# Spreading the softmax statistics of the two forward attention passes, with a longer V lag and three of sixteen K copies on ScalarE

## The chip, the cores and the metric

The kernel runs on one core of a Trainium2 chip; the other cores are idle. The metric is the device time of one execution in microseconds (us), lower is better. All runs below are of one core.

Engine names in the profile: PE is TensorE (matmuls), PEld its weight loads, DVE is VectorE, ACT is ScalarE, SPq is the queue in which SyncE issues loads. "L834" is line 834 of the kernel that the profile belongs to, so the same statement has another number in another kernel.

## The reference

Two layers, each an attention block over a long cache and a squared-ReLU feed-forward block, and then the gradient (vjp) of the whole with respect to everything but one input. Cut to what matters here:

```python
# x: [1, 1, 1024]; 32 query heads, 4 KV heads, 65536 keys, head size 128, bf16
def _A_ref(x, k_cache, v_cache, wq, wo):
    q = heads(x @ wq)
    k = jnp.repeat(k_cache, 8, axis=1);  v = jnp.repeat(v_cache, 8, axis=1)
    scores = jnp.einsum("bhqd,bhkd->bhqk", q, k) * (128 ** -0.5)
    p = _softmax(scores, axis=-1)
    return merge(jnp.einsum("bhqk,bhkd->bhqd", p, v)) @ wo

x = x + _A_ref(_layernorm(x), ...);  x = x + _B_ref(_layernorm(x), ...)   # layer 1
x = x + _A_ref(_layernorm(x), ...);  x = x + _B_ref(_layernorm(x), ...)   # layer 2
_out, _vjp = jax.vjp(_f, A_x, A_k_cache, A_v_cache, A_wq, A_wo, ...)      # and all gradients
```

There is one query token. Each KV head's K and V are read for only eight query rows, so an attention pass does little arithmetic for each byte that it loads.

## The kernel before

The kernel goes over the caches four times: forward of layer 1, forward of layer 2, backward of layer 2, backward of layer 1. Between them lie short "dense" stretches with projections and the feed-forward block. The change is confined to the two forward passes (and one line of the background products that run within them).

K and V come in blocks of 1 MB (128 partitions x 32 rows of 128), often two in one load. All loads go through one in-order queue and wait there until a slot of the on-chip arena is free.

```python
    def kv8(t, g, c8):                       # 8 rows per partition of block (t, g, hb)
        hb, j = divmod(c8, J)                # J = 32
        ...
            if i is None:
                sl = Slot("blk_" + t)
                nc.sync.dma_start(out=sl.t.rearrange("p (j d) -> p j d", d=DH), in_=half(KVIN[t], g, hb))
        ...
        return have[key].t.rearrange("p (j d) -> p j d", d=DH)[:, j:j + 8, :]
```

An *item* is 8 chunks of 128 keys. Sixteen items (128 chunks) make a *unit*, the piece over which one running maximum is taken. A pass has 16 units, so the two forward passes have 32. The pipeline runs three stages for each item, with lags in items:

```python
    FWD_LAG = TLEAD + SU // 8 + 5            # 2 + 16 + 5
    ...
        pipeline(items, [(kT, 0), (kS, TLEAD), (v8, FWD_LAG)], bg, end, holds)
```

`kT` transposes K on PE (eight 128x128 transposes into one PSUM bank), and the bank is copied to SBUF by the helper `evac`. For this kind ("kt") it always takes DVE:

```python
            evac(kt[:, :, :], pt[:, :, :], kind="kt")
```

`kS` makes the scores on PE. At the end of a unit it calls `stats`, which in one go takes the maximum over the unit and over the partitions (with two small PE steps), then eight exponentials on ACT, and then rescales the running sum:

```python
        def stats(g, su):
            ...
            ptm = ps_mv([R, P], F32)
            nc.tensor.transpose(ptm[:, :], pmn[:, :], ident_f[:, :])
            ...                                                  # DVE: min over keys, spread over a tile
            nc.tensor.matmul(pnb[:, :], lhsT=gmb[:, :], rhs=ident_f[0:R, 0:R], start=True, stop=True)
            nc.vector.tensor_copy(out=nm, in_=pnb[:])
            for h in range(R):
                nc.scalar.activation(out=E(p, g, c0, SU)[:, :, h], in_=S[:, h, :], func=ACTF.Exp,
                                     bias=negm[:, g, su, h:h + 1], scale=SCALE, accum_out=rs[:, h:h + 1])
            ...
                nc.scalar.activation(out=al[:], in_=df[:], func=ACTF.Exp)       # after the eight
                nc.vector.tensor_tensor(out=zn[:], in0=state[("z", g)][:], in1=al[:], op=ALU.mult)
                nc.vector.tensor_tensor(out=z2[:], in0=zn[:], in1=rs[:], op=ALU.add)
```

`v8` multiplies V with the exponentials into a PSUM accumulator and, at a unit's end, copies the accumulator out (`oacc`).

## Time and profile before

| | before |
|---|---|
| time, median (range) | 2040.85 us (2039.17 to 2042.13), 3 runs |
| span of the profiled run | 2038.8 us |
| forward pass 1, first transpose to last V product | 18.6 to 378.8 us |
| forward pass 2, the same | 427.6 to 778.6 us |
| rest of the span: backward passes and dense stretches | about 1330 us |

The following lines are the table of stretches of the kernel before: start and end of a stretch, its length, busy time and instructions of each engine, the mean granted PE clock (PEclk), the mean busy share of the core's 16 DMA engines (DMA share; values a little above 1 occur), and the rate.

```profile
core 0: us, PE busy (x) PEld busy (x) DVE busy (x) ACT busy (x) POOL busy (x), PEclk, DMA share, GB/s
20.00:355.00 335.00, 270.37 (x6218) 260.91 (x6216) 201.97 (x436) 92.61 (x286) 0.00 (x0) 0.92 1.01 419
355.00:400.00 45.00, 31.73 (x700) 30.62 (x697) 15.37 (x48) 8.59 (x23) 0.29 (x1) 0.81 0.87 336
400.00:435.00 35.00, 32.17 (x633) 31.12 (x631) 23.30 (x52) 12.86 (x14) 0.55 (x11) 1.00 1.02 403
435.00:455.00 20.00, 18.21 (x461) 17.77 (x457) 16.08 (x31) 7.30 (x20) 0.00 (x0) 1.00 0.43 150
455.00:755.00 300.00, 245.37 (x5611) 236.27 (x5609) 182.45 (x396) 84.06 (x266) 0.00 (x0) 0.91 1.01 419
755.00:790.00 35.00, 24.06 (x541) 23.25 (x538) 10.87 (x35) 7.43 (x22) 0.29 (x1) 0.83 0.73 278
```

The middles of the two forward passes have a DMA share of 1.01 and 419 GB/s. PE is busy 270 of 335 us there (its weight loads, PEld, overlap with that), DVE 202. So these stretches are bound by loading. Several loads are under way at a time: over the whole run a K load of 2 MB takes 19.2 us (median) from issue to landing, while its bytes alone, by my estimate from the 419 GB/s, would take 5 us. "HBM Reference" of the Trainium skill (Specifications) states about 425 GB/s for a core that streams alone, bounded by its 16 DMA engines; this trace agrees with 419. The idle DMA of these 800 us is around the passes' ends and starts (shares 0.87, 0.43 and 0.73).

The next lines are from the list of costliest groups of the kernel before (over the whole span): line, engine, operation, output and input, count, then busy us and mean ns of one, then idle time of the engine just before them and what ended most of it.

```profile
L152 DVE COPY kt<-ps_tr 128x1024 bf16<-128x1024 bf16 x909 | 603.6, 687 | 218.0 <-PE ps_tr L983 99.4
...
L852 PE MATMUL ps_sc<-L_qpad,kt 128*128 128x64 bf16 (+7 forms) x4096 | 206.7, 195 | 51.1 <-DVE kt L152 48.1
...
L149 ACT COPY kt<-ps_tr 128x1024 bf16<-128x1024 bf16 x115 | 114.3, 1013 | 172.4 <-PE ps_tr L983 172.0
```

A K copy costs 0.687 us on DVE and 1.013 us on ACT (ACT does this form in the backward passes already). The scores on L852 show 51.1 us of idle before them, 48.1 of it ended by the K copy.

These are lines of the list of waits of the kernel before, in 20 to 370 us (first pass): who waited for whom, us in total, times, the longest.

```profile
DVE zn L902 <- ACT al L900: 27.6, 8, 4.8
PE ps_sc L852 <- DVE kt L152: 27.5, 15, 3.2
...
DVE zn L902 <- ACT L_fw L938: 8.3, 3, 2.8
```

DVE stood still 27.6 + 8.3 = 35.9 us at the rescaling multiply `zn`, behind the exponentials of ACT. (On ACT's side the releaser is named by the last exponential, al or L_fw; all wait for the same queue of exponentials.)

The two waits hang together. These are lines of the timelines of PE and of DVE in the kernel before, around 105 us:

```profile
106.27 0.41 PE L852 MATMUL ps_sc<-L_qpad,kt 128*128 128x64 bf16 x8 [2.51 <-DVE kt L152]
```

```profile
105.45 0.17 DVE L902 TENSOR_TENSOR zn<-z,al 128x8 f32<-128x8 f32 x1 [2.75 <-ACT L_fw L938]
105.53 0.68 DVE L152 COPY kt<-ps_tr 128x1024 bf16<-128x1024 bf16 x1
```

PE had done its transposes by 103.8 us. DVE stood at `zn` until 105.45 us, then copied K, and the scores began at 106.27.

Finally, two lines of the timeline of PE in the kernel before, one at the end of each forward pass: start, length, what, and in brackets the idle time before it.

```profile
371.79 3.56 PE L917 MATMUL ps_acc<-arena 128*128 128x64 bf16 x64 [5.18 <-ACT L_fw L938]
```

```profile
772.11 2.13 PE L917 MATMUL ps_acc<-arena 128*128 128x64 bf16 x37 [5.18 <-ACT L_fw L938]
```

At each pass's end PE waits 5.18 us for the last unit's exponentials.

### The profile page before, as it was taken

What the parts mean: (1) busy time and instruction counts of PE and PEld (TensorE: products, weight loads), DVE (VectorE), ACT (ScalarE), POOL (GpSimd) and SP (SyncE); (2) the same over time, 40 slices, a digit from 0 to 9 for tenths busy, and PEclk for the clock granted to TensorE, in tenths of its full rate; (3) what the DMA queues carried; (4) which work ended last, traced back from release to release, by engine and by line L of the source; (5) the groups of instructions that cost most, each with busy time, mean ns of one, the idle gap of its engine ahead of it and who ended that gap; (6) DMA issues with size and microseconds to landing.
All of it is one profiled execution on the core that took longest, in us unless ns stands there. A gap on an engine that the chain in (4) does not pass through costs nothing.

```text
span 2038.8 us, 68986 instructions
## 1 busy us (share of the span) xinstructions
PE 1688.1 (83%) x30754; PEld 1358.9 (67%) x30754; DVE 1295.5 (64%) x2742; ACT 956.0 (47%) x1911; POOL 134.6 (7%) x296
## 2 busy tenths in 40 slices
PE   6888888797877886887878888989899979885997
PEld 6777777687877876776867876545555545543554
DVE  4656565466565663455464457868778868874886
ACT  1232232233223223345353446758677757763675
POOL 0000000000000000000000000111111111110121
PEclk8999889899899887988989989989889979996898
DMA  9999999879999997999999985999999999998996
GB/s 390 424 416 419 420 420 416 349 302 422 417 419 420 417 410 290 400 419 415 420 421 420 420 322 217 408 423 411 424 422 424 423 391 406 424 424 362 358 391 246
DMA packets 111544, 802.44 MB, mean 394 GB/s; under 512 B 9472, under 2 KB 9486, under 8 KB 49422
## 3 DMA queue, kind: packets, MB, share of 16 engines
q1 hardware_dynamic: 87198, 632.33, 75.7%
q0 software_dynamic: 24048, 165.70, 19.7%
q8 instruction: 240, 3.93, 0.8%
q14 instruction: 58, 0.48, 0.1%
HBM read 632.30 MB, written 165.69 MB: 391 GB/s over the span
## 4 chain that ended last, share of the span: by engine, by line
PE 52%; DMA 18%; ACT 14%; DVE 10%; issue 5%; SPq 1%; POOL 0%; DVEq 0%; POOLq 0%; ACTq 0%
PE ps_tr L834 9%; DMA arena<-in_A_v_cache_dram 8%; ACT arena L891 6%; DMA out_dram<-arena 5%; PE ps_sc L852 5%; PE ps_acc L917 5%; PE ps_tr L1094 4%; PE ps_gg L1146 4%; PE ps_tr L983 4%; ACT arena L149 4%; DVE kt L152 3%; PE ps_gg L1213 2%; PE ps_sc L1003 2%; PE ps_sc L1127 2%; ACT mv_t L510 2%
## 5 line engine op out<-in xcount | busy, mean ns | idle before, releaser
L152 DVE COPY kt<-ps_tr 128x1024 bf16<-128x1024 bf16 x909 | 603.6, 687 | 218.0 <-PE ps_tr L983 99.4
L149 ACT CAST arena<-ps_gg 128x512 bf16<-128x512 f32 (+1 forms) x893 | 468.5, 599 | 193.2 <-PE ps_gg L1146 167.5
L834 PE MATMUL ps_tr<-ident_b,arena 128*128 128x128 bf16 x4096 | 317.4, 228 | 4.4 <-issue 4.2
L152 DVE CAST arena<-ps_gg 128x512 bf16<-128x512 f32 (+1 forms) x378 | 253.8, 686 | 67.6 <-PE ps_gg L1213 29.0
L834 PEld LDWEIGHTS <-arena 128*128 128x128 bf16 x4096 | 255.3, 103 | 7.1 <-issue 6.7
L852 PE MATMUL ps_sc<-L_qpad,kt 128*128 128x64 bf16 (+7 forms) x4096 | 206.7, 195 | 51.1 <-DVE kt L152 48.1
L1146 PE MATMUL ps_gg<-GG,xt 64*128 64x512 bf16 x1024 | 213.5, 408 | 18.0 <-ACT arena L149 12.3
L856 ACT COPY S_sb<-ps_sc 128x512 f32<-128x512 f32 x64 | 38.5, 602 | 402.0 <-PE ps_sc L852 402.0
L852 PEld LDWEIGHTS <-kt 128*128 128x128 bf16 x4096 | 168.0, 100 | 59.7 <-DVE kt L152 53.6
L917 PE MATMUL ps_acc<-arena 128*128 128x64 bf16 (+4 forms) x4096 | 168.3, 201 | 42.6 <-issue 21.4
L1094 PE MATMUL ps_tr<-ident_b,arena 128*128 128x128 bf16 x2048 | 182.8, 233 | 23.2 <-DMA arena<-in_A_v_cache_dram 20.1
L891 ACT ACTIVATE arena<-S_sb,L_negm 128x128 bf16<-128x128 f32 x256 | 156.0, 1025 | 98.2 <-DVE L_negm L887 98.2
L1094 PEld LDWEIGHTS <-arena 128*128 128x128 bf16 x2048 | 132.0, 104 | 98.1 <-issue 73.2
L149 ACT COPY kt<-ps_tr 128x1024 bf16<-128x1024 bf16 x115 | 114.3, 1013 | 172.4 <-PE ps_tr L983 172.0
L917 PEld LDWEIGHTS <-arena 128*128 128x128 bf16 x4096 | 152.3, 104 | 44.6 <-issue 44.0
L983 PE MATMUL ps_tr<-ident_b,arena 128*128 128x128 bf16 x2048 | 158.4, 228 | 5.2 <-issue 4.2
L1173 PEld LDWEIGHTS <-arena 128*128 128x128 bf16 x2048 | 84.6, 100 | 108.8 <-issue 102.6
L983 PEld LDWEIGHTS <-arena 128*128 128x128 bf16 x2048 | 127.1, 103 | 19.6 <-issue 16.6
L1003 PE MATMUL ps_sc<-dOpad,kt 128*128 128x64 bf16 (+7 forms) x2048 | 107.3, 195 | 34.9 <-DVE kt L152 24.9
L891 ACT ACTIVATION_READ_ACCUMULATOR arena<-S_sb,L_negm 128x1 f32 x256 | 127.4, 497 | 0.0
L1173 PE MATMUL ps_acc<-X,arena 128*128 128x64 bf16 (+3 forms) x2048 | 120.1, 197 | 4.6 <-DMA arena<-in_A_k_cache_dram 4.6
L1127 PE MATMUL ps_sc<-DOB,kt 128*128 128x64 bf16 (+3 forms) x2048 | 117.7, 199 | 0.0
(253 smaller groups left out, 1978.2 us busy)
## 6 DMA issues: line engine op xcount, KB each, us to landing
arena<-in_A_k_cache_dram SPq DMA_DIRECT2D x88, 2048.0 KB, 19.2
arena<-in_A_v_cache_dram SPq DMA_DIRECT2D x83, 2048.0 KB, 22.1
out_dram<-arena POOLq DMA_DIRECT2D x151, 1024.0 KB, 11.5
arena<-in_A_v_cache_dram SPq DMA_DIRECT2D x76, 1024.0 KB, 24.9
arena<-in_A_k_cache_dram SPq DMA_DIRECT2D x72, 1024.0 KB, 24.8
arena<-in_B_w_dram SPq DMA_DIRECT2D x32, 896.0 KB, 7.3
arena<-in_A_wq_dram SPq DMA_DIRECT2D x22, 1024.0 KB, 20.9
arena<-in_B_w_dram SPq DMA_DIRECT2D x21, 1024.0 KB, 9.4
```

The lines of the kernel that those rows point to most:

```text
L149: nc.scalar.copy(out=out, in_=in_)
L152: nc.vector.tensor_copy(out=out, in_=in_)
L834: nc.tensor.transpose(pt[:, i, :], kb8[:, i, :], ident_b[:, :])
L852: nc.tensor.matmul(state["ps_s"][:, s:s + w, :].rearrange("p a b -> p (a b)"), lhsT=kt[:, i, :], rhs=L["qpad"][:, g, 0:w, :].rearrange("p ...
L891: nc.scalar.activation(out=E(p, g, c0, SU)[:, :, h], in_=S[:, h, :], func=ACTF.Exp, bias=negm[:, g, su, h:h + 1], scale=SCALE, accum_out=r ...
L917: nc.tensor.matmul(ps_o[:, 0:w, :], lhsT=vb8[:, i, :], rhs=E(p, g, c, w), start=(c % SU == 0), stop=(c % SU == SU - 1), skip_group_check=True)
L983: nc.tensor.transpose(pt[:, i, :], vb8[:, i, :], ident_b[:, :])
L1003: nc.tensor.matmul(state["ps_dp"][:, s:s + w, :].rearrange("p a b -> p (a b)"), lhsT=vt[:, i, :], rhs=dOpad[:, g, 0:w, :].rearrange("p a b ...
L1094: nc.tensor.transpose(pt[:, i, :], vb8[:, i, :], ident_b[:, :])
L1127: nc.tensor.matmul(state["ps_dp"][:, s:s + w, :].rearrange("p a b -> p (a b)"), lhsT=vt[:, i, :], rhs=DOB[:, g, 0:w, :].rearrange("p a b - ...
L1146: nc.tensor.matmul(pgs[h][:, :], lhsT=xt[64 * h:64 * h + 64, j1 // 8 + m, :], rhs=gg[64 * h:64 * h + 64, :, :].rearrange("p a b -> p (a b) ...
L1173: nc.tensor.matmul(ps_dq[:, 0:w, :].rearrange("p a b -> p (a b)"), lhsT=kb8[:, i, :], rhs=X[:, s:s + w, :].rearrange("p a b -> p (a b)"), ...
```

## The change

The intent is to take stalls out of PE's in-order stream in the forward passes. (1) The chain of the running maximum is spread over the five items that follow a unit, one step behind each item's transposes, so that PE always has other work between the small steps. (2) V runs three items later. (3) The exponential that gives the rescaling factor is issued before the eight long ones, and the rescaling of the sum is written at the unit's end, next to the accumulator's. (4) Three of sixteen K copies go to ACT. (5) One more yield in the background products.

```diff
-        if kind != "kt" and load["act"] + ca <= load["dve"] + cd:
+        if kind == "kta" or kind != "kt" and load["act"] + ca <= load["dve"] + cd:
             nc.scalar.copy(out=out, in_=in_)
 ...
-    FWD_LAG = TLEAD + SU // 8 + 5
+    FWD_LAG = TLEAD + SU // 8 + 8
 ...                                            # background products
+        if ps_of is ps_bg:
+            yield
         finish(ps[:, 0, :])
 ...
+    def after(n, fn):
+        TASKS.setdefault(NOW["i"] + n, []).append(fn)
 ...                                            # pipeline: tasks(i) runs after the first stage of item i
+    ACT_KT = (3, 12, 14)
 ...
-            evac(kt[:, :, :], pt[:, :, :], kind="kt")
+            evac(kt[:, :, :], pt[:, :, :], kind="kta" if c8 % SU // 8 in ACT_KT else "kt")
 ...                                            # kS: the unit's partial maximum
+                def top():
+                    nc.vector.tensor_reduce(out=pm[:, :, h0 // HB], in_=S[:, :, h0:h0 + HB], axis=AX.X, op=ALU.max)
+                after(1, top)
 ...                                            # stats, cut into five functions
+            def exps():
+                nc.vector.tensor_copy(out=nm, in_=v["pnb"][:])
+                if not first:
+                    ...
+                    nc.scalar.activation(out=al[:], in_=df[:], func=ACTF.Exp)
+                ...                             # then the eight exponentials
+            for n, fn in enumerate((lows, turn, low, spread, exps)):
+                after(n + 1, fn)
 ...                                            # v8, at a unit's end
+                    nc.vector.tensor_tensor(out=on[:], in0=ps_o[:, 0, :], in1=t[:], op=ALU.add)
+                    zn = spool.tile([P, R], F32, name="zn", tag="zn")
+                    nc.vector.tensor_tensor(out=zn[:], in0=state[("z", g)][:], in1=al[:], op=ALU.mult)
+                    z2 = spool.tile([P, R], F32, name="z2", tag="z2", bufs=3)
+                    nc.vector.tensor_tensor(out=z2[:], in0=zn[:], in1=rs[:], op=ALU.add)
 ...                                            # the last unit's division, by two more tasks (cut)
```

## The prediction

> **What bounds the kernel now.** The change touches only the two forward attention passes, about 20–379 and 428–779 us of the span (2038.8 us; median time 2040.85 us). The table of stretches shows the 16 DMA engines at share 1.01 and 419 GB/s in 20–355 and 455–755 us. The backward passes, with other compute, reach the same rate (417–424 GB/s), so it is a ceiling. "HBM Reference" of the Trainium skill (Specifications) states about 425 GB/s for a core that streams alone; this trace agrees. PE is busy 81% there, DVE 60%, ACT 28%. So these 635 us are bound by loads of K and V, whose bytes don't change. DMA idles only at the edges: 355–400 us (share 0.87), 435–455 (0.43), 755–790 (0.73), 790–820 (0.86), about 31 us together: an upper limit for the gain, and part of it is the dense phase, which the change leaves.
>
> **What the change does, costed from the trace.** Per unit (16 items; 32 units):
> - Three of 16 K copies move: 3 x 0.69 = 2.1 us less DVE, 3 x 1.01 us more ACT (what ACT takes for this form in the last pass). DVE goes from about 13 to 11 us of a 20 us unit, ACT from 6 to 9. Neither limits.
> - The statistics chain takes 2.0–2.5 us in a row (timeline), PE waiting some 1.1 us in it, then 4.85 us of exponentials. Spread over five items it no longer holds up PE's in-order stream, and three more items of lag (about 1.1 us of PE each) hide the exponentials. The rescaling no longer blocks DVE 2.7 us behind ACT (waits: zn 36 us in the first pass), so K copies and scores (27 us of waits) come sooner.
> - Removed stalls: perhaps 3–4 us of each unit's 20. Almost all turns into waiting for DMA.
>
> **What is on the critical path.** At the end of each forward pass PE waits 5.2 us for the last unit's exponentials (366.6–371.8 and 766.9–772.1 us), its V already landed. With three more items of V to do meanwhile, part is hidden: 1–3.5 us per pass, 2–7 us together. At the start of the second pass (438–453 us) the load queue waits 14 us for slots that V frees after the first exponentials (1.28 us table load, 4.9 us). The spread chain starts them about as late as now, and V starts three items later: between 3 us lost and 2 us won. The start of the first pass is saturated. The extra yield in background products is free.
>
> **Predicted: 2035 us, 8 in 10 within 2018 to 2046.** Faster by over 2%: 0.02; within 2%: 0.97; slower by over 2%: 0.01.
>
> **What would show it.** Middle of the forward passes: DMA share still 1.0, 419 GB/s, same length; PE's waits for K copies and the statistics chain gone, its idle total alike. DVE busy down about 66 us, ACT up about 97 us. PE's wait for the last exponentials of each pass 1–4 us instead of 5.2. First V product of the second pass at about the same time or up to 3 us later, DMA idle in 435–455 us alike. Backward passes alike, only shifted.
>
> **What would make it wrong.** If the scheduler orders PE's stream otherwise and the second pass starts its V products much later, idle DMA grows (5–8 us). If pairs of slots fall otherwise with the longer lag, the in-order load queue could be blocked in mid-pass. If the idle DMA at the edges depends on the stall per unit more than I think, the gain could reach 15–20 us; over 41 us (2%) would need the saturated windows to be not really saturated.

## More of the kernel before

Over both passes, 44.0 of the 48.1 us of waits for K copies are waits during which, for a part, DVE stood at `zn`, and from `zn` on it worked without a pause until the copy was done. No forward transpose of this kernel waits for a load.

## The result, and the profile after

| | before | after |
|---|---|---|
| time, median (range) | 2040.01 us (2037.02 to 2042.13), 4 runs | 2036.47 us (2035.52 to 2041.52), 4 runs |
| ratio after / before | | 0.9989, 95% interval 0.9968 to 1.0010 |
| span of the profiled run | 2038.8 us | 2034.8 us |
| DVE busy / ACT busy | 1295.5 / 956.0 us | 1240.1 / 1049.2 us |

A ratio here is the mean time of one kernel's runs over that of the other's of the same rounds, so it isn't quite the ratio of the medians. The verdict is "same": a change of a tenth of a per cent, with an interval that includes 1. The prediction of 2035 us lies 1.5 us from the median.

The same stretches, in the kernel after:

```profile
20.00:355.00 335.00, 268.93 (x6177) 257.75 (x6175) 177.23 (x390) 137.06 (x331) 0.00 (x0) 0.93 1.01 420
355.00:400.00 45.00, 32.12 (x719) 30.45 (x714) 11.82 (x43) 10.20 (x25) 0.29 (x1) 0.79 0.80 304
400.00:435.00 35.00, 31.65 (x525) 30.84 (x526) 19.31 (x45) 13.42 (x14) 0.55 (x11) 0.88 0.94 373
435.00:455.00 20.00, 19.88 (x469) 19.22 (x467) 16.51 (x32) 8.68 (x16) 0.00 (x0) 1.00 0.68 261
455.00:755.00 300.00, 239.11 (x5733) 228.25 (x5730) 160.12 (x360) 128.79 (x319) 0.00 (x0) 0.96 1.00 416
755.00:790.00 35.00, 24.66 (x593) 23.77 (x590) 9.69 (x34) 9.17 (x24) 0.29 (x1) 0.85 0.90 344
```

The middles are as before: share 1.01 and 1.00, 420 and 416 GB/s. DVE did 25 us less and ACT 44 us more in the first of them, and the DMA share and rate stayed. The ends and starts are mixed: the share falls in 355 to 400 and 400 to 435 us and rises in 435 to 455 and 755 to 790. The stretches are fixed in time while the second pass started 7 us later, so a stretch's share alone says little; the passes' own lengths are better:

| us | pass 1 | dense | pass 2 | dense | backward 1 | dense | backward 2 to the end |
|---|---|---|---|---|---|---|---|
| before | 360.2 | 48.8 | 351.0 | 52.4 | 347.3 | 70.2 | 790.3 |
| before, second profile | 359.9 | 49.5 | 348.3 | 52.7 | 347.4 | 68.4 | 790.7 |
| after | 362.0 | 52.5 | 341.6 | 51.7 | 347.4 | 67.8 | 791.8 |
| after, second profile | 368.2 | 48.4 | 345.6 | 52.2 | 353.3 | 63.7 | 789.9 |

(Passes run from the first transpose to the last V product; the second profiles are of the repeats described below.) The two forward passes sum to 711.2 and 708.2 us before and 703.6 and 713.8 us after. Two profiles of the same kernel differ by 10 us, more than the two kernels do.

The groups after, as shown for the kernel before:

```profile
L152 DVE COPY kt<-ps_tr 128x1024 bf16<-128x1024 bf16 x815 | 546.5, 687 | 288.2 <-PE ps_tr L853 123.9
...
L149 ACT COPY kt<-ps_tr 128x1024 bf16<-128x1024 bf16 x209 | 210.9, 1021 | 375.2 <-PE ps_tr L853 205.2
...
L871 PE MATMUL ps_sc<-L_qpad,kt 128*128 128x64 bf16 (+7 forms) x4096 | 213.1, 195 | 58.1 <-DVE kt L152 43.7
```

DVE has 94 copies of this form less (909 to 815) and ACT 94 more (115 to 209, counted over the whole span, so with those of the backward passes). The edit moves 3 x 32 = 96, and within the forward passes the traces show exactly 96 on ACT; in the backward passes `evac`, which there chooses the engine, gave two copies more to DVE (397 before, 399 after). The scores (L852 before, L871 now) still show 58.1 us of idle, 43.7 of it ended by the K copy.

The waits in 20 to 370 us after:

```profile
PE ps_sc L871 <- DVE kt L152: 24.7, 19, 3.3
DVE z L962 <- ACT arena L929: 22.2, 8, 3.8
...
DVE z L962 <- ACT L_fw L980: 8.1, 3, 2.7
...
PE ps_tr L853 <- DMA arena<-in_A_k_cache_dram: 3.8, 2, 2.3
```

The score products wait 24.7 us for K copies on DVE, against 27.5 before: the wait that the change should have removed is still there. DVE still stands still 22.2 + 8.1 = 30.3 us behind ACT's exponentials. It is only at the add `z` (the z2 of the code) now, and no longer at `zn`. A first direct wait of a transpose for a load shows up as well.

Why does DVE still wait? These two fences are the timeline of DVE around one unit's end, before and after.

```profile
64.08 0.17 DVE L902 TENSOR_TENSOR zn<-rs,al 128x8 f32<-128x8 f32 x1 [3.33 <-ACT al L900]
...
64.76 0.16 DVE L904 TENSOR_TENSOR z<-zn,rs 128x8 f32<-128x8 f32 x1
```

```profile
61.80 0.17 DVE L960 TENSOR_TENSOR zn<-rs,al 128x8 f32<-128x8 f32 x1 [0.40 <-ACT al L924]
64.68 0.17 DVE L962 TENSOR_TENSOR z<-zn,rs 128x8 f32<-128x8 f32 x1 [2.71 <-ACT arena L929]
64.76 0.16 DVE L952 COPY oacc<-ps_acc 128x8 f32<-128x8 f32 x1
```

The kernel text writes `zn` and `z2` after the accumulator's copy `oacc` of their unit. The built program has them in front even of the copy of the unit before: `zn` at 61.80 and `z` at 64.68, then that `oacc` at 64.76. The instruction scheduler had moved them forward when the program was built, and DVE executes in that order. So the add waits 2.71 us for the last of the eight exponentials, as `zn` had waited 3.33 us before, and the copy that frees the PSUM accumulator stands behind it.

Last, the ends of the passes, on PE's timeline after:

```profile
367.66 1.49 PE L945 MATMUL ps_acc<-arena 128*128 128x64 bf16 x29
372.93 1.87 PE L945 MATMUL ps_acc<-arena 128*128 128x64 bf16 x32 [3.78 <-ACT L_fw L980]
```

```profile
765.48 1.01 PE L945 MATMUL ps_acc<-arena 128*128 128x64 bf16 x29
770.74 1.87 PE L945 MATMUL ps_acc<-arena 128*128 128x64 bf16 x32 [4.25 <-ACT L_fw L980]
```

PE still waits for the last exponentials, 3.78 and 4.25 us instead of 5.18. The longer lag leaves V products of the unit before to be done just ahead of the pause (groups of 29), and that makes it shorter, as intended. But in the first pass the 1.4 us didn't shorten the end. The stretches of 4 us there show what else differed, before and then after:

```profile
368.00:372.00 4.00, 0.21 (x5) 0.21 (x5) 0.22 (x2) 3.76 (x16) 0.17 (x1) 0.55 1.01 411
372.00:376.00 4.00, 3.70 (x66) 3.53 (x63) 0.59 (x4) 0.00 (x0) 0.12 (x1) 0.60 0.92 380
376.00:380.00 4.00, 2.96 (x80) 2.76 (x80) 1.48 (x5) 1.87 (x2) 0.00 (x0) 1.00 0.52 213
```

```profile
368.00:372.00 4.00, 1.15 (x25) 1.17 (x23) 0.74 (x5) 3.98 (x16) 0.00 (x0) 0.50 1.02 413
372.00:376.00 4.00, 2.63 (x35) 2.34 (x35) 0.65 (x4) 0.90 (x5) 0.29 (x1) 0.50 0.79 324
376.00:380.00 4.00, 3.77 (x58) 3.29 (x58) 0.87 (x2) 1.87 (x2) 0.00 (x0) 0.50 0.51 210
```

In the kernel after, the granted clock is 0.50 until 381.4 us, 8.5 us past the end of the pause, and in the kernel before only until 375.2 us, 3.4 us past it (ends of the low spells are read from the clock records of the traces). The page "TensorE: Matmul & The Clock Gate" of the Trainium skill (Part 1) says that PE falls to half its clock after an idle window of about 3.4 us, that it needs a busy window of about 3.4 us to come back, and that the windows run freely, whatever the kernel does. The trace agrees in the lengths: the low spells in the forward passes of these two kernels' profiles last 3.4, 6.8, 10.2 or 13.7 us. It doesn't show that the last pause brings the fall: in the kernel after the low clock begins at 367.8 us, before that pause (369.1 us), and of the 24 low spells in the middles of the kernel before none has a pause of PE as long as 3.4 us in the 6.8 us ahead of it. Nor is the long low clock a mark of the change: in the second profile of the kernel before it lasted to 379.1 us, 9.3 us past the pause. The time from last score to last V product was 16.2 and 18.4 us in two profiles of the kernel before and 18.7 and 18.5 after in the first pass; in the second pass 16.1 and 15.3 before, 13.9 and 14.0 after.

At the start of the second pass the load queue waits for the first slots, before and after (issues of SPq, the time of one issue including its wait):

```profile
438.46 14.71 SPq L326 DMA_DIRECT2D arena<-in_A_k_cache_dram  x2
```

```profile
445.35 15.18 SPq L326 DMA_DIRECT2D arena<-in_A_k_cache_dram  x3
```

14.71 against 15.18 us: alike, as predicted. The first V product came 24.1 us after the first transpose before, and 23.3 after.

### The profile page after: what moved, and what is told of

The parts are those of the page before. It is cut to its first block, busy times and chain, and to the rows that moved or that the text cites. A ratio compares the mean times of both kernels' runs of the same rounds, so it can differ in the third digit from the quotient of the medians.

```text
span 2034.8 us, 68978 instructions
## 1 busy us (share of the span) xinstructions
PE 1676.8 (82%) x30754; PEld 1342.9 (66%) x30754; DVE 1240.1 (61%) x2647; ACT 1049.2 (52%) x2008; POOL 134.9 (7%) x296
## 4 chain that ended last, share of the span: by engine, by line
PE 50%; DMA 19%; ACT 16%; DVE 10%; issue 5%; POOL 0%; DVEq 0%; POOLq 0%; ACTq 0%; SPq 0%
DMA arena<-in_A_v_cache_dram 10%; PE ps_tr L853 8%; ACT arena L929 6%; PE ps_sc L871 5%; ACT arena L149 5%; PE ps_acc L945 4%; PE ps_tr L1025 4%; PE ps_gg L1188 4%; PE ps_tr L1136 4%; DMA out_dram<-arena 4%; PE ps_sc L1045 3%; PE ps_gg L1255 2%; DMA arena<-in_A_k_cache_dram 2%; DVE kt L152 2%; ACT kt L149 2%
## 5 line engine op out<-in xcount | busy, mean ns | idle before, releaser
L152 DVE COPY kt<-ps_tr 128x1024 bf16<-128x1024 bf16 x815 | 546.5, 687 | 288.2 <-PE ps_tr L853 123.9
L149 ACT COPY kt<-ps_tr 128x1024 bf16<-128x1024 bf16 x209 | 210.9, 1021 | 375.2 <-PE ps_tr L853 205.2
L853 PEld LDWEIGHTS <-arena 128*128 128x128 bf16 x4096 | 256.6, 103 | 15.5 <-issue 11.1
L871 PE MATMUL ps_sc<-L_qpad,kt 128*128 128x64 bf16 (+7 forms) x4096 | 213.1, 195 | 58.1 <-DVE kt L152 43.7
L871 PEld LDWEIGHTS <-kt 128*128 128x128 bf16 x4096 | 169.5, 100 | 70.2 <-DVE kt L152 51.2
L1136 PEld LDWEIGHTS <-arena 128*128 128x128 bf16 x2048 | 131.8, 104 | 100.6 <-issue 71.8
L945 PE MATMUL ps_acc<-arena 128*128 128x64 bf16 (+4 forms) x4096 | 162.5, 195 | 23.0 <-issue 12.9
L1025 PE MATMUL ps_tr<-ident_b,arena 128*128 128x128 bf16 x2048 | 159.2, 229 | 13.9 <-DMA arena<-in_A_v_cache_dram 7.8
L1215 PEld LDWEIGHTS <-arena 128*128 128x128 bf16 x2048 | 84.9, 100 | 119.8 <-issue 100.0
L945 PEld LDWEIGHTS <-arena 128*128 128x128 bf16 x4096 | 140.8, 100 | 25.1 <-issue 24.3
L1025 PEld LDWEIGHTS <-arena 128*128 128x128 bf16 x2048 | 127.5, 103 | 27.6 <-issue 15.2
L929 ACT ACTIVATION_READ_ACCUMULATOR arena<-S_sb,L_negm 128x1 f32 x256 | 127.8, 499 | 0.0
```

Of the source, the lines that this page charges most:

```text
L149: nc.scalar.copy(out=out, in_=in_)
L152: nc.vector.tensor_copy(out=out, in_=in_)
L853: nc.tensor.transpose(pt[:, i, :], kb8[:, i, :], ident_b[:, :])
L871: nc.tensor.matmul(state["ps_s"][:, s:s + w, :].rearrange("p a b -> p (a b)"), lhsT=kt[:, i, :], rhs=L["qpad"][:, g, 0:w, :].rearrange("p ...
L945: nc.tensor.matmul(ps_o[:, 0:w, :], lhsT=vb8[:, i, :], rhs=E(p, g, c, w), start=(c % SU == 0), stop=(c % SU == SU - 1), skip_group_check=True)
L1025: nc.tensor.transpose(pt[:, i, :], vb8[:, i, :], ident_b[:, :])
```

## The experiments

The theory to test: compute in the forward passes gets faster by the change, but both kernels' compute is already faster than the loads, so the gain turns into waiting for loads ("the loads absorb it"). The rival: the change doesn't speed up compute at all, since its new waits (the hoisted add, small PE steps between others) cost what it saves ("no gain to absorb"). The two don't exclude each other: a load limit holds whether or not the stalls were removed. A third question is which part does what. The quoted expectations give each theory's numbers in their own words.

### The same kernels again

No edit. The kernel before once, and the kernel after in five rounds on another chip.

> The kernel before, unchanged, to see how far the stage boundaries of one profile move by chance. Theory A (the saturated DMA engines hide what the change wins; only the edges of the forward passes count): saturated stretches 420 GB/s again; ends of the forward passes and the dense parts between them within 1 us of the first profile, except where the granted PE clock differs. If the boundaries move by 3 us or more, the 3 us that the changed kernel loses at the end of the first pass are chance.

> The changed kernel, unchanged, for a tighter ratio and a second profile. Theory A: ratio 0.997 to 1.000, that is 0 to 6 us faster; the second forward pass ends about 2 us sooner after its last score product than before, as in the first profile; the end of the first pass, which was 2.5 us worse at a granted clock of 0.5, is 0 to 2 us better if that clock was chance. Rival B (no gain at all in compute): the same ratio, and no difference at either end.

The kernel before took 2037.65 us. The kernel after took 2039.94 us (2033.43 to 2044.95), beside 2036.46 us (2035.67 to 2046.89, 11 runs) of the kernel before; the ratio was 1.0001 (0.9976 to 1.0027). So even the sign of the first 3.5 us is not established. The second profile of the kernel after had two spells of lower rate in pass 1 (in the three stretches of 10 us from 320 to 350 us: 393, 375 and 387 GB/s), where the first had 424, 423 and 415, and a backward pass of 353.3 instead of 347.4 us. The program was the same, so such differences are not the change's.

### Halved loads: the pace of compute with fewer bytes

Each block's load in the two forward passes fetches only the first 16 of its 32 rows per partition, and the compute reads these rows twice. All PE, DVE and ACT work stays, but not its order: the scheduler arranged it anew. In the kernel before, 1376 of the 4096 forward transposes stand in runs of 16 or more on PE; with halved loads it is 42. Between a unit's maximum and `zn`, DVE has 4 K copies in 22 of the 24 units with halved loads, and mostly 2 or 3 (0 to 4) with full ones. So these runs show the pace of the same work with fewer bytes and in another order, not that of the full kernels' compute as built. The result is wrong (relative error 0.32).

```diff
+        j = j % (J // 2) if have[key].lite else j
         return have[key].t.rearrange("p (j d) -> p j d", d=DH)[:, j:j + 8, :]
 ...
+                n = J // 2 if sl.lite else J
-                nc.sync.dma_start(out=sl.t.rearrange("p (j d) -> p j d", d=DH), in_=half(KVIN[t], g, hb))
+                nc.sync.dma_start(out=sl.t.rearrange("p (j d) -> p j d", d=DH)[:, 0:n, :], in_=half(KVIN[t], g, hb)[:, 0:n, :])
```

(The loads of pairs are cut likewise.)

> Wrong result on purpose: in the two forward passes each K and V block is loaded only by half, and compute reads that half twice, so all compute stays and the bytes halve. Theory A: the forward passes were held by DMA, so each shortens from 351 us to a compute-bound 270 to 305 us (17 to 19 us a unit), with DMA share near 0.6. Rival C (the passes were bound by compute all along, DMA share 1.0 being only queueing): they keep about 350 us.

> The same halved loads with the changed compute, wrong result on purpose. Theory A: freed of DMA the change shows its worth, 1 to 3 us a unit, each forward pass 16 to 48 us shorter than with the compute of before and the same halved loads, 30 to 95 us in all. Rival B (moving K copies to ScalarE and spreading the chain wins nothing for compute; the stall only moves to another engine or to a lower PE clock): less than 10 us in all.

The whole took 1965.38 and 1935.74 us. The next lines are the stretches of the two forward passes, from first transpose to last V product, with halved loads: first of the kernel before, then of the kernel after.

```profile
13.00:345.70 332.70, 278.80 (x6645) 268.94 (x6646) 215.05 (x462) 96.78 (x305) 0.29 (x1) 0.95 0.75 258
395.90:707.00 311.10, 266.38 (x6585) 257.32 (x6583) 214.69 (x459) 97.96 (x306) 0.29 (x1) 0.97 0.74 251
```

```profile
12.90:319.20 306.30, 267.87 (x6644) 259.71 (x6645) 183.20 (x414) 144.99 (x354) 0.29 (x1) 0.99 0.79 280
371.00:675.00 304.00, 262.16 (x6586) 254.49 (x6584) 182.70 (x411) 146.47 (x354) 0.29 (x1) 0.98 0.74 257
```

The DMA share is 0.74 to 0.79 at 251 to 280 GB/s, so loads no longer bind. The passes are 332.7 + 311.1 = 643.8 us before and 306.3 + 304.0 = 610.3 us after. Without the load limit the change gains 33.5 us, which is 1.05 us for each of the 32 units, so in this form the rival falls. With full loads the same passes take 711.2 and 703.6 us, in both kernels longer than with halved loads. That fits the theory: fewer bytes make both kernels faster, and the change's gain shows only then.

Two things are not shown by it. The builds differ in order as well as in bytes, so a part of the difference can be order. And that removed stalls turn into *waiting for loads* is not seen in the full kernels: in 20 to 355 us PE was busy 270.37 us before and 268.93 after, its idle time is still put down mostly to K copies and the steps of the maximum, and the forward transposes' direct waits for loads are 3.8 us. With full loads the stalls were hardly removed, which leaves the rival standing beside the load limit there. What holds for any order is the rate: in all seven profiles with full loads, 20 to 340 and 455 to 745 us have a DMA share of 0.99 to 1.01 at 408 to 420 GB/s, and the bytes are the same.

I had thought compute in the kernel before faster than it is: I expected passes of 270 to 305 us and measured 333 and 311. That is only 8% and 11% less than the passes take with full loads (360.2 and 351.0 us).

Where do the 33.5 us come from? PE busy time falls from 278.80 + 266.38 = 545.2 to 530.0 us though it does the same products, and idle time from 98.6 to 80.3 us. So about half is fewer idle microseconds and about half is the same work in less time. The second half goes with the granted clock, which rises from 0.95 to 0.99 in the first pass and from 0.97 to 0.98 in the second. That the clock is the cause of it is argued: I did no run that holds the clock fixed.

These lines are groups of the two runs with halved loads: score products and V products on PE, with the idle time before them.

```profile
L858 PE MATMUL ps_sc<-L_qpad,kt 128*128 128x64 bf16 (+7 forms) x4096 | 209.0, 193 | 10.0 <-issue 8.9 <-DVE kt L152 0.8
L923 PE MATMUL ps_acc<-arena 128*128 128x64 bf16 (+4 forms) x4096 | 194.6, 195 | 57.9 <-ACT al L906 22.7 <-issue 14.4 <-ACT L_fw L944 14.4
```

```profile
L877 PE MATMUL ps_sc<-L_qpad,kt 128*128 128x64 bf16 (+7 forms) x4096 | 204.8, 192 | 4.6 <-issue 3.5 <-DVE kt L152 1.0
L951 PE MATMUL ps_acc<-arena 128*128 128x64 bf16 (+4 forms) x4096 | 200.2, 194 | 54.3 <-DVE oacc L964 19.9 <-DVE oacc L958 13.4 <-ACT L_fw L986 9.8
```

Two things are to be seen. First, the idle time of the score products before, 51.1 us with full loads, is 10.0 us with halved loads, and the part put down to K copies falls from 48.1 to 0.8 us. No edit touched DVE between these two runs, so one is tempted to call the wait the load limit seen second-hand. The traces don't bear that out. As shown above, 44.0 of the 48.1 us are waits that go back to DVE's stand at `zn`, with the transposes done. With halved loads the order is another: DVE's idle time before `zn` falls from 78.7 to 28.8 us over both passes, and none of it lies in a wait of the scores for K copies. So "PE waits for DVE" was right for the full kernel, and DVE waited for ACT's exponentials. Second, the V products' idle time, 57.9 us before, is mostly behind exponentials (22.7 + 14.4). In the changed kernel it is 54.3 us, and now mostly behind `oacc` (19.9 + 13.4), the copy that frees the accumulator and stands behind the hoisted add. One wait was exchanged for another.

### Which part does what, with halved loads

Each is the changed kernel with halved loads and one part undone (one execution each, wrong), except the last, which is the kernel before with only the lag added. `lite_zlate` makes the hoisting impossible: it writes the accumulator's copy into z2 first, so that the rescaling has to follow it.

```diff
 # lite_nolag
-    FWD_LAG = TLEAD + SU // 8 + 8
+    FWD_LAG = TLEAD + SU // 8 + 5
 # lite_noact
-    ACT_KT = (3, 12, 14)
+    ACT_KT = ()
 # lite_nospread
-                after(1, top)
+                top()
-                after(n + 1, fn)
+                fn()
 # lite_zlate
-                    zn = spool.tile([P, R], F32, name="zn", tag="zn")
-                    nc.vector.tensor_tensor(out=zn[:], in0=state[("z", g)][:], in1=al[:], op=ALU.mult)
                     z2 = spool.tile([P, R], F32, name="z2", tag="z2", bufs=3)
-                    nc.vector.tensor_tensor(out=z2[:], in0=zn[:], in1=rs[:], op=ALU.add)
+                    nc.vector.tensor_copy(out=z2[:], in_=on[:])
+                    nc.vector.tensor_tensor(out=z2[:], in0=state[("z", g)][:], in1=al[:], op=ALU.mult)
+                    nc.vector.tensor_tensor(out=z2[:], in0=z2[:], in1=rs[:], op=ALU.add)
 # lite_lagonly: kernel before
-    FWD_LAG = TLEAD + SU // 8 + 5
+    FWD_LAG = TLEAD + SU // 8 + 8
```

> Halved loads, changed compute but with the old lag of V (three items shorter); wrong result on purpose. The two forward passes (first transpose to last V product) took 333 + 311 us with the compute of before and 306 + 304 us with the changed one. If the longer lag, which lets PE work while ScalarE does the exponentials, is what the change wins: 630 us or more in sum. If it is worth little: 615 us or less.

> Halved loads, changed compute but all K copies on VectorE; wrong result on purpose. VectorE is busy 62% in the passes of the changed kernel and would go to about 72%, still not the limit: 610 to 618 us for the two passes against 610. If moving K copies were the main gain: 630 us or more.

> Halved loads, changed compute but the statistics chain of a unit issued in one go after its last scores, as before, with the longer lag and the moved copies; wrong result on purpose. If the spreading matters for PE's in-order stream: 620 to 635 us for the two passes against 610. If the instruction scheduler had already interleaved the chain with other work: 610 to 614 us.

> Halved loads, changed compute, and the rescaling of the sum tied to the unit's accumulator (a copy of it is written first into the tile of the sum, so that no scheduler can move the rescaling ahead); wrong result on purpose. In the changed kernel the list of VectorE instructions shows the rescaling hoisted to just after the negated maximum, where it waits about 2 us for the exponentials and holds up the copy of the accumulator, for which PE waits 1.7 us. Theory: that wait goes, 24 units x 0.5 to 1.7 us, so 570 to 598 us for the two passes against 610. Rival: PE's own work and other waits take it up, 605 us or more.

> Halved loads, compute of before with one edit, the lag of V three items longer; wrong result on purpose. With the old lag the two forward passes took 644 us in both forms (compute of before and changed), with the whole change 610 us. If the lag alone is the gain, this takes 600 to 615 us; if it needs the spreading or the moved copies beside it, 625 us or more.

| halved loads | whole, us | pass 1 | pass 2 | sum |
|---|---|---|---|---|
| before | 1965.38 | 332.7 | 311.1 | 643.8 |
| changed | 1935.74 | 306.3 | 304.0 | 610.3 |
| changed, lag undone | 1970.39 | 333.8 | 310.0 | 643.8 |
| changed, no copies on ACT | 1937.14 | 304.6 | 303.7 | 608.3 |
| changed, chain in one go | 1923.98 | 301.7 | 300.4 | 602.1 |
| changed, rescaling tied to the end | 1930.42 | 303.8 | 300.5 | 604.3 |
| before, lag alone | 1939.58 | 309.5 | 307.0 | 616.5 |

The lag is what makes the change pay. Alone it brings 643.8 - 616.5 = 27.3 of the 33.5 us, and without it nothing is left. The copies on ACT do nothing that can be seen (2 us in the wrong direction). Spreading the chain costs about 8 us: with it in one go, both passes are shorter. From lag alone (616.5) to the changed kernel with its chain in one go (602.1) there are another 14 us, from the rescaling, the earlier small exponential, the ACT copies and the extra yield together. Tying the rescaling to the end brings 6 us.

Why spreading costs shows in the V products' group of that run:

```profile
L951 PE MATMUL ps_acc<-arena 128*128 128x64 bf16 (+4 forms) x4096 | 200.2, 194 | 27.2 <-ACT L_fw L986 9.8 <-issue 8.9 <-DVE oacc L964 4.6
```

Its idle time is 27.2 us against 54.3, and the part behind `oacc` L964 4.6 against 19.9. Spread, the exponentials start five items later, so the add that waits for them blocks the accumulator's copy just when the next unit's V products want the bank. In one go, they have the time. The last two steps of this are argued from the lines shown, not tested by themselves. The expectations were met for the lag undone (630 us or more, 643.8 measured), nearly met for no copies on ACT (610 to 618) and the lag alone (600 to 615), and missed for the other two: the chain in one go came out below both of its ranges (the lowest began at 610 us), and the rescaling came out above its predicted 570 to 598 us. The differences of 2 to 8 us come from one execution each, and each of these builds can have an order of its own. I take the size of the lag's effect as settled; for the smaller ones I rely on both passes moving the same way.

### The better compute with full loads

`calm` is the changed kernel with the chain in one go and the rescaling tied to the end, with full loads and a correct result. If the passes were bound by more than the loads, it should gain. `edge` is `calm` with two more edits that aim at the idle DMA at the start of a pass: an exponential on a dummy ahead of the pass, so that the table is loaded early, and single-block loads for the first 20 blocks instead of 10.

```diff
 # calm: lite_nospread and lite_zlate's edits, without halved loads
 # edge: calm, and
         items = ITEMS[p]
+        warm = tmp.tile([P, 1], F32, name="warm")
+        nc.scalar.activation(out=warm[:], in_=L["rstd"][:], func=ACTF.Exp)
 ...
-        KV["halves"] = set(TOUCH[p][-8:] + (TOUCH[p][:10] if p else []))
+        KV["halves"] = set(TOUCH[p][-8:] + (TOUCH[p][:20] if p else []))
```

> Full loads, right result: the changed kernel with the statistics chain issued in one go and the rescaling tied to the accumulator, the two edits that won 8 and 6 us of 610 with halved loads. Theory A (DMA holds the passes): ratio to before within 0.997 to 1.000, the saturated stretches at 419 GB/s and share 1.0 as before. Rival (compute sets the pace of the full passes): 10 to 14 us faster than the changed kernel, ratio 0.993 or less.

> Right result: the former, and two edits at the start of the second pass, where the load queue waits some 15 us for pairs of slots: its first 20 blocks, not 10, are loaded one slot at a time, and the exponential's table is loaded ahead (1.28 us). Theory A: only idle DMA time can be won, so 2 to 8 us against before, ratio 0.996 to 0.999, with the DMA idle between the start of the second pass and the first V product down from 9 us by some microseconds. If the order of slots elsewhere suffers: ratio 1.000 or above.

`calm` took 2047.55 us (2044.01 to 2053.72), ratio 1.0050 (1.0030 to 1.0069): half a per cent slower, and the interval excludes 1. `edge` took 2042.09 us (2038.46 to 2045.44), ratio 1.0018 (1.0001 to 1.0036). The kernel before beside them took 2037.70 us (2031.82 to 2042.99, 11 runs). So the version that was 8 and 6 us better in two single tests with halved loads gains nothing when loads bind, as the theory says; that it loses, the theory doesn't say, and the expectations of both runs were missed (0.997 to 1.000 and 0.996 to 0.999 by the theory; `edge` fell into its alternative, 1.000 or above if the order of slots elsewhere suffers, which I did not look into).

The trace of `calm` shows one wait exchanged for another. This is its group of score products; the longer list of groups goes on with 17.5 us behind DVE's K copies:

```profile
L871 PE MATMUL ps_sc<-L_qpad,kt 128*128 128x64 bf16 (+7 forms) x4096 | 217.3, 197 | 53.0 <-ACT kt L149 32.0
```

DVE no longer waits for exponentials at the rescaling, and the scores' waits for DVE's K copies are 17.5 us, against 43.7 in the changed kernel. But those for K copies on ACT are 32.0 us, against 11.4: where the eight exponentials are issued in one go, a K copy on ACT stands behind them (at 83.75 us right after the last one, and the scores wait 2.84 us for it). With halved loads neither part alone had shown a wait of the scores for K copies on ACT, so the halved-load runs didn't foretell it.

`edge` did what its edits aimed at: the DMA share in 435 to 460 us rose to 0.98 (371 GB/s) from 0.67 (251) in the changed kernel and 0.54 (203) before. The total didn't follow. Its two dense stretches around the second pass took 54.4 and 55.7 us, against 48.8 and 52.4 before.

What else shows in `calm` is a lower clock in the dense stretches. This is the stretch from 380 to 440 us, of `calm` and then of the last kernel below:

```profile
380.00:440.00 60.00, 49.21 (x928) 47.54 (x928) 23.74 (x68) 16.22 (x22) 0.84 (x12) 0.82 0.77 298
```

```profile
380.00:440.00 60.00, 52.59 (x1013) 51.18 (x1010) 30.42 (x74) 14.27 (x16) 0.55 (x11) 0.89 0.91 351
```

At a clock of 0.82 against 0.89, less is done and less is loaded. Over the profiles with full loads, the dense stretch after pass 1 was 48.4 and 48.8 us where its clock was 0.93 and 0.90, and 54.4 and 55.0 us at 0.84. The one profile of `calm` also has dips of the load rate in the middle of pass 1 (346 GB/s in 290 to 300 us), where the in-order load queue issued nothing from 279.12 to 293.54 us. All three are seen; which of them makes it slower in all its runs, and why its clock is lower, stays open.

### The lag alone, with full loads

The kernel before with a single constant changed.

```diff
-    FWD_LAG = TLEAD + SU // 8 + 5
+    FWD_LAG = TLEAD + SU // 8 + 8
```

> Full loads, right result: the kernel before with one edit, the lag of V three items longer, which with halved loads gave 27 of the 34 us of the whole change. Theory A (DMA holds the full passes): ratio to before 0.998 to 1.001, saturated stretches at 419 GB/s as before. If compute set the pace anywhere but at the edges: 0.990 or less. If the longer lag by itself makes the in-order load queue run dry in mid-pass or lengthens the ends of the passes: 1.002 or more.

It took 2032.96 us (2030.84 to 2035.84, 6 runs), beside 2039.83 us (2027.40 to 2046.60, 11 runs) of the kernel before; the ratio was 0.9965 (0.9936 to 0.9993). The result is correct. The ratio lies just below the theory's range (0.998 to 1.001). It is the only kernel whose interval lies below 1, and it does it without the rest of the diff. Its passes sum to 358.9 + 343.3 = 702.2 us, near the 703.6 of the changed kernel's first profile. It was not run beside the changed kernel, so that it beats it is likely and not shown.

## Why the prediction was right

The number and the class were right (2035 us predicted, 2036.47 measured; within 2%). Point by point:

- *The forward passes are bound by loads, and removed stalls turn into waiting for loads.* The first half is right: the middles kept their share (1.01, 1.00) and rate (420, 416 GB/s), and with halved loads both kernels' passes got shorter. The second half is not shown: 33.5 us of gain appear with halved loads and not with full ones, but in another order of instructions, and with full loads most stalls were still there rather than turned into waits for loads (3.8 us of these).
- *Only the edges can gain, 2 to 7 us at the ends of the passes.* The wait for the last exponentials fell to 3.78 and 4.25 us, within or just over the predicted 1 to 4. What came of it was less: nothing in the first pass, where PE ran at half clock for some 8.5 us after the pause (9.3 us in one of the two profiles before, 3.4 in the other), and about 1.8 us on average in the second. I hadn't reckoned with the clock. Over both rounds of runs the net gain isn't distinguishable from zero.
- *Start of the second pass alike.* Right: 14.71 and 15.18 us of waiting in the load queue, the first V product 0.8 us earlier.
- *DVE down about 66 us, ACT up about 97.* Measured 55.4 down and 93.2 up.
- *Removed stalls, 3 to 4 us of each unit's 20.* Too large by a factor of three to four, as far as halved loads can tell: 33.5 us over the two passes are 1.05 us for each of the 32 units. The step that failed is the list of what removes them. The three items of lag do nearly all; the spread chain, which I had counted as the first cause, costs some 8 us; and about half of the gain is the same work in less time, which goes with the clock.
- *The rescaling no longer blocks DVE.* Wrong: 35.9 us of waiting at `zn` became 30.3 us at `z`. I read the order in the kernel's text, and the scheduler had another.
- *PE's waits for K copies gone.* Wrong: 27.5 became 24.7 us. The cause that the prediction named was right: 44.0 of 48.1 us over both passes go back to DVE's stand at `zn`. But the rescaling still blocked DVE, now at `z`; and in `calm`, where it didn't, 32.0 us of waits for K copies on ACT came in their place.

None of the three errors is seen in the total: all are about compute in stretches where the DMA engines were busy all the time. In part that is luck: a middle held by loads gives the same number whether the stalls were removed or not, and here most were not. Had the passes been bound by compute, 3 to 4 us per unit would have meant some 100 us promised and 33 delivered.

## What to carry to other kernels

Before you make the compute of a stretch faster, look at its DMA share; where it is 1.0 at the rate that other stretches reach too, halve the loads (with a wrong result) and you learn in one run how far the same work can go with fewer bytes. But compare the order of instructions before you carry a wait from one build to the other: here the scheduler changed it with the loads. Which waits are real is read in the full trace, by asking what the engine that is named waited for itself. Undo the parts of a change one at a time in that mode: here one constant did most of the work of the whole diff, and one of the other parts worked against it. Check in the trace, not in the source, where the scheduler put an instruction that is meant to come late.

## What the Trainium skill lacked or had wrong

- "TensorE: Matmul & The Clock Gate", Part 1, held in the lengths of the low spells (3.4 to 13.7 us). What it says first of their cause, an idle window of about 3.4 us, didn't hold: 24 of 24 low spells in the middles of the kernel before came without a pause of PE that long just ahead. That is nearer to its passage on a second failure mode, where short idle times suffice. It says that the ramp costs under 1% of a typical kernel's span; here the clock fell again and again, and its mean over the profiled run of the kernel before was 0.903.
- "ScalarE: Activation LUTs" (What ACT_TABLE_LOAD costs) gives 1283 ns for the load and 1380 ns for a drain with it. The load took 1.28 us here; no drain is to be seen, the first exponential starts right behind it (load at 445.50, exponential at 446.79 us).
- The same section gives the cost of an ACTIVATE without an accumulator output, and I found no page that names ScalarE's separate accumulator read (the VectorE pages name DVE's): in the kernel after, 256 of them took 127.8 us, 0.499 us each, beside exponentials of 1.019 us that overlap with each other.
- "Perfetto Trace Analysis" (What "DMA-bound" means) lists engines, the issuing sequencer and SBUF reads. It lacks the in-order load queue that waits for a buffer to come free (elsewhere the page speaks only of bubbles of an engine where too few buffers can be allocated): 14.71 us at the start of the second pass with the DMA share at 0.43 over 20 us.
